# Fourier mixing and a quick-GELU layer on one Trainium2 core: ScalarE's partition moves reissued later, and the first products of a group on one PSUM bank

## The chip, the cores and the metric

The kernel runs on one core of one Trainium2 chip, in one launch. The metric is the device time in microseconds of that core. Before the change three runs took 2061.47, 2064.64 and 2069.29 us; their median is 2064.64 us. The profile shown below is one execution with a span of 2067.7 us.

## The reference

```python
batch, seq, dim = (8, 3008, 256)                     # x, float32
X = np.fft.fft(x, axis=1)
X = np.fft.fft(X, axis=2)
x = X.real.astype(np.float32).reshape(B * S, D)      # 24064 x 256
h = x @ w_in                                         # 256 x 2048
g = h * (1.0 / (1.0 + np.exp(-1.702 * h)))
return (g @ w_out).astype(np.float32)                # 2048 x 256
```

Everything is float32: the real part of a two-dimensional Fourier transform of each of eight samples, and then a layer with one hidden width of 2048 and a sigmoid-weighted activation.

## The kernel before

**What is computed how.** The transform along the sequence (3008 = 47 x 64) is done in two stages by matrix products, with the symmetry of a real input used to halve the work. The transform along the features is folded into the first weight, so that the hidden layer comes out of two products, P with the cosine half of the weight (wcs0) and Q with the sine half (wcs1). Since a row and its mirrored row share P and Q, one pass gives hidden values for both: P + Q forward and P - Q backward. The second layer uses a Winograd form of the 2 x 2 block product: seven products of sums and differences in place of eight. For most of the work two of these seven are split once more in the same way (the "deep" form); the parts of the two are the "small products", which lie in partitions 0 to 63 for the one and 64 to 127 for the other.

**Steps, groups and slots.** The work is a list of 384 steps: 8 samples, 3 blocks each, 2 halves of a block, and 8 steps (NP) in each half, each of which covers 256 of the 2048 hidden columns. The 8 steps of one half accumulate into the same PSUM banks and make a *group*; there are 48 groups. The loop at L906 walks over slots t. In slot t the hidden layer of step t is made, and the second-layer products of step t - 3 (LAG = 3) are issued. So a new group's products begin in the slots with t mod 8 = 3. Below, "slot 3" means a slot with t mod 8 = 3, and so on; slot 3 is the *boundary slot*. The first group (t below 8) is plain, groups 2 to 47 are deep, and the last group is not deep.

**What a slot holds, in the order in which it is issued.** There is no scheduler: each engine's queue has the instructions in the order in which this loop writes them.

- TensorE (all its products but the small ones are issued by the helper at L478): `second(t)` adds Q onto P in the step's bank (8 passes; a float32 product takes two passes, and each is cut into two column halves); `product(t - 3, 0)`, the first two of the five full-size products; `begin(t + 1)`, the next step's P; `product(t - 3, 1)`, the other three; then the small products at L623 (16 passes in even slots, 12 in odd ones).
- ScalarE: `middle(t + 2)`, two scalings (L542); `forward(t)`, the activation of P + Q (L555), which waits for `second(t)`; `activate_back(t - 1)`, the activation of the mirrored half (L562).
- VectorE: `backward(t)` (L503), which makes P - Q; `doubled(t + 1)` (L548), which reads P of the next step and writes 2P plus a row term into SBUF; `second(t + 1)` on TensorE may not add Q before it has done so; then the sums s2 and s4 (L577, L578) and those of the small products (L595).
- GpSimd: the sums s1 and s3 (L574, L575), and in the first third of a sample the folding of the next sample's input (`fold1`, L201 to L206).

`backward(t)` waits for `forward(t)`: both write the same tile h, and both read the same PSUM bank.

**How a group ends.** Five full-size products go to three banks: pot[0] holds (0,0) and (0,1), pot[1] holds (1,0) and (1,1), pot[2] holds (2,0). In the pair, the first number is the bank and the second its half. The small products lie in pot[3] and pot[4].

- `combine(t)`, at the end of slot 2, where the group's last products were issued: ScalarE copies c1 out of pot[0] (L697); four VectorE additions (L703) follow, u2 (reads pot[0]), u3 (reads pot[1]), c (reads pot[1]) and one that reads pot[2].
- `combine_small(t)`, one slot later, at the end of slot 3: ScalarE copies the sum e out of pot[4] (L721); four VectorE additions (L727) combine the small products into the tile held[3]; three ScalarE copies (L728 to L730) exchange a quarter in partitions 0 to 63 with one in partitions 64 to 127.
- `combine_last(t, 0)`, at the end of slot 4: VectorE adds held[3] to the rest (L739), transposes a half (L677) and stores it; `combine_last(t, 1)`, at the end of slot 5, does the other half.

The three banks of the full-size products have no double: the next group's first products in slot 3 go to the banks that `combine` reads. The order of the five products of a step is written out by hand:

```python
plan = [(0, 0, wo[:, p, 0, :], h[:, 0, 0, :n]), (1, 0, wt[:, p, 2, :], s[:, 2, :n]),
        (0, 1, wt[:, p, 1, :], s[:, 1, :n]), (1, 1, wt[:, p, 0, :], s[:, 0, :n]),
        (2, 0, wo[:, p, 3, :], s[:, 3, :n])]
todo = plan[:2] if part == 0 else plan[2:]
```

In some slots more is issued at the end: the next block's second transform stage (L332, with VectorE transposes L338) in slot 0 of every other group, and the next sample's first stage (`mix1`, L230, with two ScalarE copies out of PSUM, L233). In the samples 1 to 6 (counted from 0) `mix1` falls into slots 2 and 6 of the second and third group of the sample. One of its two banks is that of the step just finished, so that it is also the bank of `begin` in the next slot.

Of the kernel before, what the change touches and what calls it, by code (L numbers as in the profile page):

```python
# [43 lines left out]
LAG = 3  # L44
# [67 lines left out]
def kernel(ctx: ExitStack, tc, x, w_in, w_out, tab1, tab2, out):  # L112
    nc = tc.nc
# [29 lines left out]
    wo, wt = wot[:, 0], wot[:, 1]  # L143
# [318 lines left out]
    NP = NF // 2  # L462
    steps = [(b, blk, hh, p) for b in range(B) for blk in range(NBLK) for hh in range(2) for p in range(NP)]
    vb, ht, st, rt, xb, gt, pot = {}, {}, {}, {}, {}, {}, {}
    held = []
    last = len(steps) - NP

    def width(t):

        return 226 if steps[t][1:3] == (0, 1) else 256  # L470
# [52 lines left out]
    def begin(t):  # L523

        n = width(t)
        x = xb[t] = bank("x", f"b{t % 2}")
        for i in range(2):
            halves(x[:, i * 256:i * 256 + n], *operands(t, 0, i), start=(i == 0), stop=False)
# [35 lines left out]
    def sums(t, eng):  # L564

        if not NP <= t < len(steps):
            return
        h, n = ht[t], width(t)
        a11, a12, a21, a22 = h[:, 0, 0, :n], h[:, 0, 1, :n], h[:, 1, 0, :n], h[:, 1, 1, :n]
        if eng is nc.gpsimd:  # L570
            st[t] = held[2] if t % 4 == 3 else sp.tile([128, 4, 256], F32, tag="s", bufs=3, name="s")
        s1, s2, s3, s4 = (st[t][:, q, :n] for q in range(4))
        if eng is nc.gpsimd:
            eng.tensor_tensor(s1, a21, a22, op=ALU.add)  # L574
            eng.tensor_tensor(s3, a11, a21, op=ALU.subtract)  # L575
        else:
            eng.tensor_tensor(s2, s1, a11, op=ALU.subtract)  # L577
            eng.tensor_tensor(s4, a12, s2, op=ALU.subtract)  # L578

    def deep(t):  # L580

        return NP <= t < last
# [16 lines left out]
    def sub(k):  # L599
        q, at = SUBS[k]  # L600
        return pot[q][:, at * 128:(at + 1) * 128]
# [36 lines left out]
    def product(t, part):  # L638

        p, n = steps[t][3], width(t)  # L640
        if part == 0 and p == 0:
            for q in range(2 if t < NP else 3):
                pot[q] = bank(f"po{q}", f"o{q}")
            if t >= NP and not deep(t):
                pot[5] = bank("po5", "b2" if deep(t - 1) else "o3")
        h = ht[t]
        if t < NP:

            plan = [(half, dh, wo[:, p, 2 * f + dh, :], h[:, half, f, :n])
                    for half in range(2) for dh in range(2) for f in range(2)]  # L650
        else:
            s = st[t]
            plan = [(0, 0, wo[:, p, 0, :], h[:, 0, 0, :n]), (1, 0, wt[:, p, 2, :], s[:, 2, :n]),
                    (0, 1, wt[:, p, 1, :], s[:, 1, :n]), (1, 1, wt[:, p, 0, :], s[:, 0, :n]),
                    (2, 0, wo[:, p, 3, :], s[:, 3, :n])]
            if not deep(t):
                plan += [(2, 1, wo[:, p, 2, :], h[:, 0, 1, :n]), (5, 0, wt[:, p, 3, :], h[:, 1, 1, :n])]
        todo = plan[:2] if part == 0 else plan[2:]

        if t >= len(steps) - 2:  # L660
            if part == 0:
                return
            pot[t] = plan
            if t == len(steps) - 2:
                return
            todo = [it for both in zip(pot.pop(t - 1), pot.pop(t)) for it in both]
        begun = set() if p else pot.setdefault("begun", set())
        for q, i, lhs, rhs in todo:
            halves(pot[q][:, i * 256:i * 256 + n], lhs, rhs, start=(p == 0 and q not in begun), stop=(p == NP - 1))
            begun.add(q)  # L670
        if part and p == 0:
            del pot["begun"]
# [7 lines left out]
    def combine(t):  # L680

        b, blk, hh, p = steps[t]
        if p < NP - 1:
            return
        n = width(t)
        o = op.tile([128, 4, 256], F32, tag="os", name="os")
        if t < NP:
            for half in range(2):
                turned(t, o, half, pot[half][:])
            return  # L690
        c = cv.tile([128, 4, 256], F32, tag="m", bufs=2, name="c")
        if n < 256:
            nc.gpsimd.memset(c[:, :, n:], 0.0)
        m = {k: pot[q][:, 256 * i:256 * i + n] for k, q, i in ((6, 0, 1), (7, 1, 0), (5, 1, 1), (3, 2, 0))}
        u = op.tile([128, 3, 256], F32, tag="u", bufs=1, name="u")
        c1, u2, u3 = (u[:, q, :n] for q in range(3))
        nc.scalar.copy(c1, pot[0][:, 0:n])  # L697
        m5 = free(pot[1][:], 256, [0, 2], [1, n])
        plan = [(u2, c1, m[6], ALU.add), (u3, u2, m[7], ALU.add),
                (free(c[:], 256, [512, 2], [1, n]), u[:, 1:3, :n], m5, ALU.add),  # L700
                (c[:, 1, :n], c[:, 1, :n], m[3], ALU.add)]
        for out_, i0, i1, how in plan:
            nc.vector.tensor_tensor(out_, i0, i1, op=how)  # L703
        pot["late"] = o, c, u
        if deep(t):
            return
        for out_, i0, i1, i in ((c[:, 0, :n], c1, pot[2][:, 256:256 + n], 0), (c[:, 2, :n], u3, pot[5][:, 0:n], 1)):
            nc.vector.tensor_tensor(out_, i0, i1, op=ALU.add)
            turned(t, o, i, c[:, 2 * i:])

    def combine_small(t):

        if t < 0 or not deep(t) or steps[t][3] < NP - 1:
            return
        n, w, d = width(t), width(t) // 2, held[3]
        e, saved = d[:, 896:896 + w], d[:, 768:]

        def two_of(ap, at, by):
            return free(ap[:], at, [by, 2], [1, w])

        nc.scalar.copy(e, sub(1)[:, :w])  # L721
        d22 = d[:, 256 + w:256 + 2 * w]
        for out, i0, i1 in ((two_of(d, 0, 512), two_of(d, 896, 0), two_of(pot[3], 0, 128)),
                            (two_of(d, 640, 128), two_of(d, 512, 0), two_of(pot[3], 256, 128)),
                            (two_of(d, 256, w - 256), two_of(d, 640, 128), two_of(pot[4], 0, 128)),
                            (d22, d[:, 768:768 + w], sub(5)[:, :w])):
            nc.vector.tensor_tensor(out, i0, i1, op=ALU.add)  # L727
        nc.scalar.copy(saved[64:128, :n], d[0:64, 256:256 + n])  # L728
        nc.scalar.copy(d[0:64, 256:256 + n], d[64:128, 0:n])  # L729
        nc.scalar.copy(d[64:128, 0:n], saved[64:128, :n])  # L730
# [175 lines left out]
    for t in range(n + LAG):  # L906
        if t < NP:
            hidden(t)
            if t == 0:
                low_up(in2)  # L910
                nyquist(0, 0)
                low_down(in2)
            if t in rows_at:
                first_row(rows_at[t])
            if t >= LAG:
                for part in range(2):
                    product(t - LAG, part)
            if t in early:
                fold_w(early[t])
            if t:  # L920
                activate(t - 1)
            rows(t)
            if t == NP - 1:
                for ahead in range(2):
                    middle(NP + ahead)
                begin(NP)
        else:
            if t < n:
                if t + 2 < n:
                    middle(t + 2)  # L930
                second(t)
            product(t - LAG, 0)
            if t + 1 < n:
                begin(t + 1)
            product(t - LAG, 1)
            small_products(t - LAG, (1, 2, 4, 7))
            small_products(t - LAG - 1, (5, 6, 3))
            if t == NP:
                activate(t - 1)
            if t < n:  # L940
                forward(t)
            if NP < t <= n:
                activate_back(t - 1)
                sums(t - 1, nc.gpsimd)
            if t < n:
                backward(t)
        if NP <= t + 1 < n:
            doubled(t + 1)
        if t >= NP:
            sums(t - 2, nc.vector)  # L950
            deeper(t - 2, 0)
            deeper(t - 3, 1)
        if t >= LAG:
            combine(t - LAG)
            combine_small(t - LAG - 1)
            combine_last(t - LAG - 2, 0)
            combine_last(t - LAG - 3, 1)
        if t == NP:
            held += [hp.tile(shape, F32, tag="h", name="held") for shape in
                     ([128, 2, 4, 2, 64], [128, 2, 4, 2, 64], [128, 4, 256], [128, 1024])]  # L960
        if t >= NP:
            spare[:] = ["b2", f"b{t % 2}"]
        for fn, args in extra.get(t, ()):
            fn(*args)
# [28 lines left out]
```

## Time and profile before

| engine | busy us | share of the span |
|---|---|---|
| TensorE matmuls (PE) | 1928.9 | 93% |
| TensorE weight loads (PEld) | 1399.4 | 68% |
| VectorE (DVE) | 1548.5 | 75% |
| ScalarE (ACT) | 875.3 | 42% |
| GpSimd (POOL) | 796.1 | 38% |

The span is 2067.7 us, with 51061 instructions; the mean granted TensorE clock is 0.986 of full speed. The DMA engines are lightly used (51 GB/s on average). The busy time of PE is modelled from pipelined matmuls, so that a span in which PE never waits shows as fully busy; the missing 7% are the time in which it stood.

The chain of work that ended last is followed back from the last instruction, at each step to what released it. By engine it consists of PE 70%, DVE 17%, ACT 7% and a small rest. Where it leaves PE, PE stood and another engine's work set the time.

### The profile page before, as it was taken

What the parts mean: (1) busy time and instruction counts of PE and PEld (TensorE: products, weight loads), DVE (VectorE), ACT (ScalarE), POOL (GpSimd) and SP (SyncE); (2) the same over time, 40 slices, a digit from 0 to 9 for tenths busy, and PEclk for the clock granted to TensorE, in tenths of its full rate; (3) what the DMA queues carried; (4) which work ended last, traced back from release to release, by engine and by line L of the source; (5) the groups of instructions that cost most, each with busy time, mean ns of one, the idle gap of its engine ahead of it and who ended that gap; (6) DMA issues with size and microseconds to landing.
All of it is one profiled execution on the core that took longest, in us unless ns stands there. A gap on an engine that the chain in (4) does not pass through costs nothing.

```text
span 2067.7 us, 51061 instructions
## 1 busy us (share of the span) xinstructions
PE 1928.9 (93%) x21392; PEld 1399.4 (68%) x21392; DVE 1548.5 (75%) x3011; ACT 875.3 (42%) x1868; POOL 796.1 (38%) x1073
## 2 busy tenths in 40 slices
PE   8989999989998999999999999999999999999998
PEld 5666677667676676666666666666666666677665
DVE  7667778777788777787778777788777877777775
ACT  6533434444444444444444344434444444444442
POOL 4474224532245322452225522255222642322232
PEclk9999999999999999999999999999999999999999
DMA  8623151236220352204513054031631222202201
GB/s 284 130 45 43 51 81 14 44 46 112 17 35 23 53 106 17 47 16 75 81 15 52 16 100 54 12 57 39 95 31 22 17 44 44 26 13 17 20 18 22
DMA packets 145399, 104.93 MB, mean 51 GB/s; under 512 B 104914, under 2 KB 127986, under 8 KB 143984
## 3 DMA queue, kind: packets, MB, share of 16 engines
q1 hardware_dynamic: 143952, 101.14, 29.3%
q8 instruction: 168, 2.75, 0.6%
q10 hardware_dynamic: 1216, 0.52, 0.1%
q14 instruction: 63, 0.52, 0.1%
HBM read 58.38 MB, written 48.01 MB: 51 GB/s over the span
## 4 chain that ended last, share of the span: by engine, by line
PE 70%; DVE 17%; ACT 7%; issue 2%; DMA 1%; POOL 1%; SPq 1%; DVEq 0%; ACTq 0%; POOLq 0%
PE po L478 31%; PE x L478 26%; PE po L623 10%; DVE r L595 3%; DVE held L727 3%; DVE g L548 3%; ACT g L542 2%; DVE h L503 2%; ACT h L555 1%; DVE c L703 1%; PE ps L230 1%; PE ps L332 1%; DVE s L577 1%; DVE u L703 1%; ACT held L729 1%
## 5 line engine op out<-in xcount | busy, mean ns | idle before, releaser
L478 PE MATMUL x<-pq,wcs 128*64 128x256 f32 (+1 forms) x6016 | 789.1, 382 | 84.5 <-DVE g L548 82.3
L478 PE MATMUL po<-s,wo 128*64 128x256 f32 (+1 forms) x4512 | 586.5, 379 | 27.8 <-DVE c L703 25.3
L478 PEld LDWEIGHTS x<-pq,wcs 128*64 128x64 f32 x6016 | 433.6, 139 | 260.5 <-DVE g L548 94.5
L555 ACT ACTIVATE h<-x 128x512 f32<-128x512 f32 (+1 forms) x376 | 220.2, 586 | 749.9 <-PE x L478 729.8
L574 POOL TENSOR_TENSOR s<-h 128x256 f32<-128x256 f32 (+1 forms) x282 | 204.9, 727 | 792.9 <-issue 460.8
L503 DVE TENSOR_TENSOR h<-g,x 128x512 f32<-128x512 f32 (+2 forms) x440 | 254.5, 590 | 330.2 <-ACT h L555 329.5
L478 PEld LDWEIGHTS po<-s,wo 128*64 128x64 f32 x4512 | 344.0, 139 | 178.9 <-issue 40.9
L542 ACT ACTIVATE g<-nb,af 128x256 f32<-128x256 f32 (+1 forms) x752 | 335.1, 495 | 1.4 <-DVE h L512 0.8
L548 DVE SCALAR_TENSOR_TENSOR g<-x,g 128x512 f32<-128x512 f32 (+1 forms) x376 | 254.4, 677 | 95.0 <-PE x L478 94.7
L478 PE MATMUL po<-h,wo 128*64 128x256 f32 (+1 forms) x1824 | 267.6, 382 | 2.5 <-DVE u L703 2.2
L562 ACT ACTIVATE h<-h 128x512 f32<-128x512 f32 (+1 forms) x376 | 230.9, 614 | 0.2 <-DVE h L503 0.2
L574 POOL TENSOR_TENSOR held<-h 128x256 f32<-128x256 f32 (+1 forms) x94 | 69.9, 744 | 404.1 <-ACT h L562 319.3
L575 POOL TENSOR_TENSOR s<-h 128x256 f32<-128x256 f32 (+1 forms) x282 | 206.6, 733 | 0.0
L595 DVE TENSOR_TENSOR r<-h 128x256 f32<-128x256 f32 (+1 forms) x368 | 195.8, 573 | 0.0
L478 PE MATMUL po<-held,wo 128*64 128x256 f32 (+1 forms) x1504 | 193.0, 375 | 0.0
L623 PE MATMUL po<-r,held 128*64 128x128 f32 (+1 forms) x2208 | 184.4, 270 | 0.0
L478 PEld LDWEIGHTS po<-h,wo 128*64 128x64 f32 x1824 | 134.5, 138 | 71.7 <-DVE u L703 17.8
L577 DVE TENSOR_TENSOR s<-s,h 128x256 f32<-128x256 f32 (+1 forms) x282 | 168.8, 598 | 3.1 <-POOL s L574 3.1
L623 PEld LDWEIGHTS po<-r,held 128*64 128x64 f32 x2208 | 143.4, 137 | 22.0
L578 DVE TENSOR_TENSOR s<-h,s 128x256 f32<-128x256 f32 (+1 forms) x282 | 147.8, 524 | 9.7
L478 PEld LDWEIGHTS po<-held,wo 128*64 128x64 f32 x1504 | 110.8, 137 | 49.0
L623 PE MATMUL po<-h,wo 128*64 128x128 f32 (+1 forms) x1472 | 112.1, 271 | 2.5 <-DVE held L727 2.2
(106 smaller groups left out, 1700.8 us busy)
## 6 DMA issues: line engine op xcount, KB each, us to landing
out_dram<-os SPq DMA_DIRECT2D x284, 64.0 KB
Td<-xt SPq DMA_DIRECT2D x14, 768.0 KB
t<-Td SPq DMA_DIRECT2D x7, 1536.0 KB
xt<-in_x_dram SPq DMA_DIRECT2D x14, 512.0 KB
xt<-Xr SPq DMA_DIRECT2D x14, 512.0 KB
nb<-pq SPq DMA_DIRECT2D x23, 256.0 KB
out_dram<-os SPq DMA_DIRECT2D x96, 56.0 KB
Xr<-in_x_dram SPq DMA_DIRECT2D x7, 752.0 KB
```

What stands on the lines that cost most here:

```text
L478: nc.tensor.matmul(out[c0:c0 + 64], lhsT=lhs[:, c0:c0 + 64], rhs=rhs, skip_group_check=True, **how)
L503: nc.vector.tensor_tensor(free(h[:], 512 + at + m - 1, [256, 2], [RUN, blocks], [-1, m]), *ins, op=op)
L542: nc.scalar.activation(g[:, i * 256:i * 256 + n], nbt[b, blk][:, hh * 256:hh * 256 + n], ACTF.Copy, scale=af2[:, f:f + 1])
L548: nc.vector.scalar_tensor_tensor(g, two(xb[t][:], n), 2.0, g, op0=ALU.mult, op1=ALU.add)
L555: nc.scalar.activation(two(h[:], n), two(xb[t][:], n), ACTF.Gelu_apprx_sigmoid)
L562: nc.scalar.activation(g, g, ACTF.Gelu_apprx_sigmoid)
L574: eng.tensor_tensor(s1, a21, a22, op=ALU.add)
L575: eng.tensor_tensor(s3, a11, a21, op=ALU.subtract)
L577: eng.tensor_tensor(s2, s1, a11, op=ALU.subtract)
L578: eng.tensor_tensor(s4, a12, s2, op=ALU.subtract)
L595: nc.vector.tensor_tensor(out, i0, i1, op=how)
L623: nc.tensor.matmul(sub(k)[64 * side:64 * side + 64, :w], lhsT=lhs, rhs=rhs, start=(p == 0 and k in (1, 2)), stop=(p == NP - 2), skip_group ...
```

## The change

Three edits. First, in `combine_small` the copy of e moves forward: it is now issued in `combine`, one slot earlier, behind the copy of c1. Second, the three exchanging copies get a function of their own, `swap`, which is called one slot later than before, behind that slot's `forward` and `activate_back`, and ahead of `backward`. Third, the five products of a step are reordered so that the first two both go to pot[0], and in a boundary slot `begin(t + 1)` is issued ahead of `product(t - 3, 0)`. The first two edits are for ScalarE: its queue should not stand at the copies while activations wait behind them. The third is for TensorE: it should not stand at pot[1] while VectorE still reads it. No instruction is added or removed, and every engine has the same instructions as before, in another order on TensorE and ScalarE; the order on VectorE, GpSimd and SyncE does not change.

```diff
-            plan = [(0, 0, wo[:, p, 0, :], h[:, 0, 0, :n]), (1, 0, wt[:, p, 2, :], s[:, 2, :n]),
-                    (0, 1, wt[:, p, 1, :], s[:, 1, :n]), (1, 1, wt[:, p, 0, :], s[:, 0, :n]),
+            plan = [(0, 0, wo[:, p, 0, :], h[:, 0, 0, :n]), (0, 1, wt[:, p, 1, :], s[:, 1, :n]),
+                    (1, 0, wt[:, p, 2, :], s[:, 2, :n]), (1, 1, wt[:, p, 0, :], s[:, 0, :n]),
                     (2, 0, wo[:, p, 3, :], s[:, 3, :n])]
...
         if deep(t):
+            nc.scalar.copy(held[3][:, 896:896 + n // 2], sub(1)[:, :n // 2])
             return
...
-        nc.scalar.copy(e, sub(1)[:, :w])
         d22 = d[:, 256 + w:256 + 2 * w]
...
             nc.vector.tensor_tensor(out, i0, i1, op=ALU.add)
+
+    def swap(t):
+
+        if t < 0 or not deep(t) or steps[t][3] < NP - 1:
+            return
+        n, d = width(t), held[3]
+        saved = d[:, 768:]
         nc.scalar.copy(saved[64:128, :n], d[0:64, 256:256 + n])
         nc.scalar.copy(d[0:64, 256:256 + n], d[64:128, 0:n])
         nc.scalar.copy(d[64:128, 0:n], saved[64:128, :n])
...
-            product(t - LAG, 0)
-            if t + 1 < n:
-                begin(t + 1)
+            heads = [(product, t - LAG, 0)] + [(begin, t + 1)] * (t + 1 < n)
+            for fn, *args in heads[::-1] if t >= NP + LAG and (t - LAG) % NP == 0 else heads:
+                fn(*args)
             product(t - LAG, 1)
...
                 activate_back(t - 1)
                 sums(t - 1, nc.gpsimd)
+            swap(t - LAG - 2)
             if t < n:
                 backward(t)
```

More of the change, by code (lines that the diff above doesn't have):

```diff
@@ L714, in combine_small @@
             return
-        n, w, d = width(t), width(t) // 2, held[3]
-        e, saved = d[:, 896:896 + w], d[:, 768:]
+        w, d = width(t) // 2, held[3]
         def two_of(ap, at, by):
             return free(ap[:], at, [by, 2], [1, w])
-        nc.scalar.copy(e, sub(1)[:, :w])
         d22 = d[:, 256 + w:256 + 2 * w]
```

## The prediction

> **What bounds the kernel now.** I read the page first. PE is busy 93% of the span and heads the chain of work with 70%, so the question is where the other 30% of the chain lie. The list of waits gives the times in which PE stood, and for whom:
>
> ```profile
> ACT held L728 <- DVE held L727: 101.6, 46, 4.1
> ...
> PE x L478 <- DVE g L548: 82.3, 52, 3.0
> ...
> PE po L478 <- DVE c L703: 25.3, 40, 0.7
> ```
>
> Columns: total us, times, longest us. PE stood 107.6 us in two places, about once in each of the 46 ends of a deep group (46 is the count of L728). Then the chain of waits, in order of time, over one such end:
>
> ```profile
> 1037.70 0.43 DVE u L703
> ...
> 1038.15 0.70 DVE c L703
> ...
> 1038.99 0.65 PE po L478 x4
> ...
> 1042.49 0.28 ACT held L721
> ...
> 1044.47 0.41 ACT held L728
> ...
> 1045.76 0.91 ACT g L542 x2
> 1046.66 0.49 ACT h L555
> ...
> 1047.18 0.69 DVE h L503
> 1047.87 0.61 DVE g L548
> ```
>
> Columns: start us, us, what. Twice the chain leaves PE. *Stall A*, in boundary slot 3: product (1,0) waits until c has been read out of pot[1]. *Stall B*, in slot 4: ScalarE stands at the exchanging copies (L728 waits for L727); behind them in its queue are `middle` and `forward`; VectorE waits for `forward`, and PE for VectorE's `doubled`. Last, windows cut at the starts of slots 3 and 4, in an ordinary group and in one with `mix1` (its slots 4 and 5):
>
> ```profile
> 1036.60:1042.25 5.65, 4.95 (x52) 3.41 (x50) 4.76 (x11) 1.12 (x2) 1.41 (x2) 1.00 0.38 16
> 1042.25:1048.52 6.27, 4.96 (x56) 3.94 (x52) 3.25 (x9) 4.18 (x10) 0.72 (x2) 1.00 0.02 4
> ...
> 914.33:922.29 7.96, 4.96 (x58) 3.83 (x53) 5.10 (x10) 4.09 (x10) 3.78 (x5) 0.95 0.00 0
> 922.29:929.81 7.52, 7.52 (x48) 4.53 (x50) 5.74 (x11) 1.91 (x4) 5.01 (x7) 0.60 0.15 32
> ```
>
> Columns: length, then busy us of PE, PEld, DVE, ACT, POOL, then clock, DMA share, GB/s. An undisturbed odd slot is 0.86 + 0.86 + 0.86 + 1.29 + 0.67 = 4.54 us by the chain's own pieces; the even slot 2 before this boundary took 4.76. So A costs 5.65 - 4.54 = 1.11 us and B 6.27 - 4.76 = 1.51 us, restart of the pipeline included. In the mix group B is longer, and after a 3.00 us stop the clock is down to 0.60 in slot 5.
>
> **What the Trainium skill says.** "PSUM — Partial Sum Buffer", section "PSUM bank collisions raise a hardware error", wants PSUM guarded by bank and quadrant, not by address: this is why (1,0) waits for c, and why giving the first two products to pot[0] alone moves the wait from c to u2. The trace agrees: (0,0) started at 1037.65, when u2 was made, and (1,0) 1.34 us later. The same page, "Engine vs sequencer instructions", calls the queues of ScalarE and VectorE strictly first in, first out; stall B is that. "TensorE: Matmul & The Clock Gate", section "What's actually happening", has the clock at half after an idle window of some 3.4 us; the trace shows 0.60 after a stop of 3.00 us and 1.00 after the 1.31 us of the ordinary B. "SBUF — State Buffer", section "Who interferes with whom", says that a VectorE operation with two SBUF inputs contends with GpSimd's reads; here L595 takes 494 ns for 256 columns on average but 948 ns for 226, whose groups coincide with GpSimd's folding.
>
> **The change part by part**, in times after the start of slot 3 (1036.60 in the ordinary case). No instruction is added, so no work is priced, only waits and margins.
>
> *Products on one bank, behind P (stall A).* PE: `second` to 0.86, `begin` to 1.72, (0,0) and (0,1) to 2.58, then (1,0). VectorE works without a break from 1034.65 on, so its times stand: u2 at 1.05, c at 2.25, the reader of pot[2] at 2.76, where PE arrives at 3.44. All three are in time, the tightest by 0.33 us. Product (0,1) now needs s2 in every slot, 1.29 us after `second` begins (0.43 more in slot 3, and 0.86 for P); s2 is VectorE's next operation after the `doubled` that releases `second`, and takes 0.4 to 0.8, 1.1 at worst. So no new wait: A's 1.11 us go. `begin` in front needs the bank of step t - 1, which VectorE left 2 us earlier; behind it wait only the products.
>
> *Copy of e one slot earlier.* It waits for the small products of slot 2 and so ends at about 0.3; behind it ScalarE has `middle` (0.91), so `forward` starts at 1.25 in place of 1.08. VectorE is in `combine` until 2.76, which hides it. In return L727 loses the copy's 0.28 us ahead of it.
>
> *The exchange one slot later (stall B).* VectorE: `backward` from 2.76 to 3.4, `doubled` to 4.05 (PE's next `second` is due at 4.54), sums to 4.9, L595 to 5.6, L727 (1.60 for four) to 7.2. ScalarE in slot 4: `forward` from 5.5 to 6.1, `activate_back` to 6.7, then it waits for L727 and copies from 7.2 to 8.5. VectorE: `backward` (0.69) and `doubled` (0.61) from 7.2 to 8.5; PE wants that at 4.54 + 4.76 = 9.30. Margin 0.8 us, B's 1.51 go. The small products of slot 4, which overwrite what L727 reads, come at 8.4: margin 1.2. The added wait, L739 on the exchange, has `backward` and `doubled` of slot 5 behind it on VectorE, and PE behind these; VectorE gets there after its sums at 10.5, 2 us after the copies' end, so it costs nothing.
>
> *Ordinary boundaries:* 46 less 12 with `mix1` = 34, times 2.62 = 89 us. Check: 34 x (0.68 + 1.31) us of standing = 68, which leaves 40 of the 107.6, or 3.3 each, for the other 12; the long B of the window says the same.
>
> *The 12 mix boundaries.* Here `mix1`'s copies (L233) keep `forward` of slot 3 until 911.8, and GpSimd's folding stretches two L595 to 2.36. From `backward` at 911.82 VectorE has 0.69 + 0.6 + 0.82 + 0.35 + 2.36 + 1.48 (L727) + 0.69 + 0.61 = 7.6 us, so `doubled` ends at 919.4 in place of 922.25. PE is there at about 918.8: `begin`, now in front, must wait some 0.4 us (and a 0.2 restart) for the L233 copy that holds its bank until 910.50. So 0.6 us of stop remain, and the saving is 2.9; in the other of the two kinds the same sum gives 2.6. I take 2.7: 12 x 2.7 = 32 us. The stop is too short for the clock to fall. The clock's loss is (1 - 0.986) x 2068 = 29 us, of which start and end have about 5; of the other 24 I count 15, since VectorE would have bound some of the slow slots anyway.
>
> *Sum:* 89 + 32 + 15 = 136 us. I take 4 off for small new waits (0.1 in each boundary): 2064.6 - 132 = 1932 us.
>
> **The rivals.** *VectorE becomes the bound.* It is busy 4.76 + 3.25 + 4.49 = 12.5 us in slots 3 to 5, against 13.89 for PE undisturbed. GpSimd's two additions of a slot can double an operation with two SBUF inputs (0.41 to 0.8); in a new phase three more of them would use up 1.2 us against margins of 0.33 and 0.8. For: the margins are small. Against: in the windows shown these operations are already hit once a slot, and after slot 5 VectorE catches up. It would leave about 1 us at each of 46 boundaries: 1932 + 46 = 1978.
>
> *Only A goes.* If `swap` held ScalarE as long as before, or L739 took over the wait, B would stay. Then 34 x 1.1 and some of the mix groups: 2064.6 - 45 = 2020. For: the copies still wait for L727 in ScalarE's queue. Against: `forward` and `activate_back` are now in front, and only the next `middle` is behind, due 2 us later.
>
> *Slower.* `begin` in front waits for L233 or a backlog on VectorE in every boundary, and L739 holds VectorE for the whole exchange in slot 4, with `doubled` behind it; if both cost 1.5 us where A and B cost 2.6 and the freed stalls came back one slot later, the kernel would end at 2064.6 + 46 x 0.4 = 2083. The margins above speak against it.
>
> **How the numbers follow.** Both stalls gone 0.70, VectorE bound 0.17, only A 0.09, slower 0.04. The time is that of the likeliest, 1932. The lowest that the trace allows is 2064.6 less 112 us of standing (both waits, with 4.4 on u and L727), some 20 of restarts (92 x 0.2) and 24 of clock: 1909. The low end is 1911, and the upper end 1985, to take in VectorE as the bound; the other two cases, 0.13, stay outside with a little of the first. Faster by over 0.5%: 0.95; the same 0.02; slower 0.03.
>
> **What would show it.** In the profile after, "PE po <- DVE c" and L728's wait ahead of `forward` should be gone, "PE x <- DVE g" should fall from 82 to 20 us or less, PE should rise to 97 or 98%, and ordinary slots 3 and 4 should take 4.5 and 4.8 us. Slot 3 at 4.9 or more would say that (1,0) or `begin` waits; slot 5 longer than 4.7, that L739 does. A clock that still falls in the mix groups would leave 15 us. The prediction is wrong if VectorE's busy time grows by more than a few per cent through contention with GpSimd.

## The result and the profile after

The changed kernel takes 1927.78 us (median of four runs, 1925.14 to 1927.89) against 2066.86 us before (median of four: the three runs named at the start and one of 2069.08): a ratio of 0.9327, with a 95% interval of 0.9305 to 0.9350. The forecast was 1932 us.

In the list of waits of the changed kernel (total us, times, longest us), the two lines that were stall A and stall B read as follows. L734 and L726 are the L728 and L727 of before, and the line "PE po <- DVE c" is gone from the list.

```profile
ACT held L734 <- DVE held L726: 17.0, 22, 1.3
...
PE x L478 <- DVE g L548: 4.6, 7, 0.8
```

PE stood 107.6 us for VectorE in these two places; 4.6 are left. The exchange still waits for L726, now and then, but with nothing behind it that is due. The chain of waits over the same stretch of an ordinary group (start us, us, what), from the `second` of slot 3 to the end of slot 4, no longer leaves PE:

```profile
1007.49 1.73 PE x L478 x16
1009.22 2.16 PE po L478 x20
1011.38 0.66 PE po L623 x12
...
1015.92 0.87 PE po L623 x16
```

The first line is `second` and the `begin` drawn in front of the products, 16 passes in one piece; the second is all five products; the pieces left out are PE's as well. Then the windows (length, busy us of PE, PEld, DVE, ACT, POOL, then clock, DMA share, GB/s): slots 3 and 4 of this ordinary group, and slots 4 and 5 of a mix group of the same kind as the one shown of before.

```profile
1007.32:1011.86 4.54, 4.54 (x52) 3.25 (x50) 4.23 (x10) 2.98 (x7) 1.43 (x2) 1.00 0.00 2
1011.86:1016.62 4.76, 4.76 (x56) 3.46 (x54) 4.59 (x12) 3.23 (x7) 1.43 (x2) 1.00 0.02 3
```

```profile
858.97:863.73 4.76, 4.76 (x57) 3.46 (x55) 4.62 (x10) 2.44 (x6) 4.35 (x6) 1.00 0.00 0
863.73:868.27 4.54, 4.54 (x53) 3.24 (x51) 4.40 (x10) 2.64 (x6) 2.19 (x4) 1.00 0.12 27
```

Both boundary slots are down to an undisturbed slot: 5.65 and 6.27 us became 4.54 and 4.76. In the mix group 7.96 and 7.52 became 4.76 and 4.54, and the clock stays at 1.00 where it was 0.60. The page's first part says the same for the whole span; the chain is 83% PE in place of 70%.

```profile
PE 1892.3 (98%) x21392; PEld 1376.7 (71%) x21392; DVE 1549.2 (80%) x3011; ACT 875.6 (45%) x1868; POOL 786.5 (41%) x1073
```

VectorE's busy time did not grow (1548.5 before, 1549.2 after). PE's fell by 36.6 us, though it has the same 21392 passes: fewer of them ran at the low clock (mean granted clock 0.986 before, 0.996 after), and fewer began again after a stop (the four passes behind stall A took 0.65 us; four in the run of 20 above take 0.43).

If the span is cut at the first pass of each `second`, the 141.6 us by which the profiled span fell (2067.7 to 1926.1) divide into 90.5 us in the 34 groups with an ordinary boundary, 50.4 us in the 12 mix groups (those whose boundary has a `mix1`) and 0.8 us elsewhere, each rounded.

### The profile page after: what moved, and what is told of

Read it like the earlier page. It is cut to its first block, busy times and chain, and to the rows that moved or that the text cites. A ratio compares the mean times of both kernels' runs of the same rounds, so it can differ in the third digit from the quotient of the medians.

```text
span 1926.1 us, 51018 instructions
## 1 busy us (share of the span) xinstructions
PE 1892.3 (98%) x21392; PEld 1376.7 (71%) x21392; DVE 1549.2 (80%) x3011; ACT 875.6 (45%) x1868; POOL 786.5 (41%) x1073
## 4 chain that ended last, share of the span: by engine, by line
PE 83%; DVE 11%; ACT 3%; POOL 1%; issue 1%; DMA 0%; SPq 0%; DVEq 0%; ACTq 0%; POOLq 0%
PE po L478 37%; PE x L478 29%; PE po L623 12%; DVE r L595 4%; DVE h L503 2%; DVE g L548 1%; PE ps L332 1%; PE ps L230 1%; DVE s L577 1%; DVE s L578 1%; ACT xt L233 1%; DVE held L577 1%; PE ps L283 1%; ACT g L542 1%; DVE os L677 1%
## 5 line engine op out<-in xcount | busy, mean ns | idle before, releaser
L478 PE MATMUL x<-pq,wcs 128*64 128x256 f32 (+1 forms) x6016 | 771.5, 377 | 9.0 <-DVE g L548 4.6
L555 ACT ACTIVATE h<-x 128x512 f32<-128x512 f32 (+1 forms) x376 | 221.5, 589 | 793.1 <-PE x L478 697.3
L478 PE MATMUL po<-s,wo 128*64 128x256 f32 (+1 forms) x4512 | 571.6, 375 | 3.0 <-DVE s L577 1.9
L478 PEld LDWEIGHTS x<-pq,wcs 128*64 128x64 f32 x6016 | 426.7, 137 | 180.8 <-issue 12.3
L478 PEld LDWEIGHTS po<-s,wo 128*64 128x64 f32 x4512 | 334.0, 137 | 150.6 <-DVE s L577 2.3
L595 DVE TENSOR_TENSOR r<-h 128x256 f32<-128x256 f32 (+1 forms) x368 | 205.1, 598 | 0.0
L578 DVE TENSOR_TENSOR s<-h,s 128x256 f32<-128x256 f32 (+1 forms) x282 | 133.3, 473 | 9.7
```

The source lines that it names most:

```text
L478: nc.tensor.matmul(out[c0:c0 + 64], lhsT=lhs[:, c0:c0 + 64], rhs=rhs, skip_group_check=True, **how)
L555: nc.scalar.activation(two(h[:], n), two(xb[t][:], n), ACTF.Gelu_apprx_sigmoid)
L595: nc.vector.tensor_tensor(out, i0, i1, op=how)
```

## The experiments

All are the changed kernel with one thing put back, moved or multiplied, unless the text says otherwise. "After" in what follows is the changed kernel, which took 1928.24 us when it was run once more beside the first two kernels of the last part, on the mix groups (ratio 0.9347, 0.9333 to 0.9361). Each ratio is to runs of the kernel before made beside it (medians from 2063.62 to 2067.09 us), so kernels that were not run side by side are best compared by their ratios.

### Each half of the change alone

Products and P in the new order, ScalarE's copies where they were:

```diff
         if deep(t):
-            nc.scalar.copy(held[3][:, 896:896 + n // 2], sub(1)[:, :n // 2])
             return
...
+        nc.scalar.copy(d[:, 896:896 + w], sub(1)[:, :w])
         d22 = d[:, 256 + w:256 + 2 * w]
...
-            swap(t - LAG - 2)
...
             combine_small(t - LAG - 1)
+            swap(t - LAG - 1)
```

> The third edit alone (products reordered, P ahead in the boundary slot); the copy of e and the exchange stay where they were before. My theory: the two stalls lie one behind the other, so this edit alone is worth less than stall A's 1.11 us. PE leaves slot 3 after 4.54 us, but VectorE still ends L727 7.2 us after the slot's start (its own work, not the copy of e, sets this), the exchange ends at 8.5, the scalings at 9.4, the activation at 10.0, P - Q at 10.6 and `doubled` at 11.2: slot 4 grows from 6.27 to about 6.7, and an ordinary boundary gains 0.67, not 1.11 us. 34 x 0.67 = 23 us and nothing in the mix groups, whose clock still falls: 2067 - 23 = 2044 us. Rival, each edit takes its own stall: slot 4 stays at 6.27 and the time is 2067 - 34 x 1.11 = 2029 us.

Measured: 2024.76 us, ratio 0.9819 (0.9791 to 0.9846). The time alone would speak for the rival's 2029, but the windows of an ordinary group do not: slot 3 lost its stall and slot 4 grew.

```profile
1051.05:1055.59 4.54, 4.54 (x52) 3.25 (x50) 4.23 (x10) 1.11 (x2) 1.42 (x2) 1.00 0.01 2
1055.59:1062.12 6.53, 4.93 (x56) 3.39 (x52) 3.60 (x10) 4.18 (x10) 0.72 (x2) 1.00 0.01 3
```

And the chain over another ordinary boundary of this kernel shows why: VectorE comes to L726 straight from its own sums, and no copy of e and no PE stands ahead of it.

```profile
1016.79 0.67 DVE r L595 x2
1017.46 0.34 DVE held L726
...
1018.35 0.63 DVE held L726 x2
...
1019.06 0.41 ACT held L734
...
1022.45 0.61 DVE g L548
```

So an ordinary boundary gained 1.11 us in slot 3 and gave back 0.26 in slot 4, 0.85 in all: between my 0.67 and the rival's 1.11. L726 ended sooner than I had put it (at 1018.98, when slot 3 had begun at 1012.05: after 6.9 us, not 7.2). Over all 34 of these groups the profiled run gained 29 us. Its span is another 19 us shorter, of which 17.5 are in the mix groups, mostly from a clock that fell less often there (0.994 in the profiled run; over the four, 0.994 and 0.995 in the two runs of 2021 and 2023 us, 0.990 and 0.989 in those of 2027 and 2031). Neither theory had foreseen that.

The moves on ScalarE alone, products and P in the old order:

```diff
-            plan = [(0, 0, wo[:, p, 0, :], h[:, 0, 0, :n]), (0, 1, wt[:, p, 1, :], s[:, 1, :n]),
-                    (1, 0, wt[:, p, 2, :], s[:, 2, :n]), (1, 1, wt[:, p, 0, :], s[:, 0, :n]),
+            plan = [(0, 0, wo[:, p, 0, :], h[:, 0, 0, :n]), (1, 0, wt[:, p, 2, :], s[:, 2, :n]),
+                    (0, 1, wt[:, p, 1, :], s[:, 1, :n]), (1, 1, wt[:, p, 0, :], s[:, 0, :n]),
...
-            heads = [(product, t - LAG, 0)] + [(begin, t + 1)] * (t + 1 < n)
-            for fn, *args in heads[::-1] if t >= NP + LAG and (t - LAG) % NP == 0 else heads:
-                fn(*args)
+            product(t - LAG, 0)
+            if t + 1 < n:
+                begin(t + 1)
```

> The first two edits alone (e early, exchange one slot later), with the products and P in the old order. My theory: stall B goes wholly, since slot 3 stays at 5.65 us and VectorE then has even more time: slot 4 4.76, slot 5 4.54. 34 x 1.51 = 51 us from ordinary boundaries, and nearly all of the mix groups' gain (about 50 us, the clock no longer falls): about 1967 us. PE waits for `c` about 25 us, as before. Rival, stall B returns in part as a wait of L745 for the exchange or of slot 5: slot 4 or slot 5 over 5 us and a time over 1990.

Measured: 1977.7 us, ratio 0.9580 (0.9562 to 0.9599). The windows of slots 3 and 4 of an ordinary group, and the line of waits for stall A:

```profile
1033.36:1039.03 5.67, 4.98 (x53) 3.50 (x50) 4.78 (x11) 2.98 (x7) 1.42 (x2) 1.00 0.00 1
1039.03:1043.79 4.76, 4.76 (x57) 3.99 (x55) 4.31 (x11) 3.23 (x7) 1.43 (x2) 1.00 0.01 3
```

```profile
PE po L478 <- DVE c L703: 25.3, 40, 0.7
```

Stall A is there as before, to the tenth of a microsecond, and stall B is gone. The time is 11 us over my 1967, which had the mix groups gain some 50 us; they gained 40 (slot 4 takes 5.74 us there in the one kind, against 4.49 after). The two halves bring 39.8 and 86.9 us by their medians, 126.7 together; the change brings 139 (135 in the later comparison). Part of the difference is what the first half gives back as long as the second is missing: 34 x 0.26 = 9 us.

### Which part of the new order counts

The new order of products without P ahead:

```diff
-            heads = [(product, t - LAG, 0)] + [(begin, t + 1)] * (t + 1 < n)
-            for fn, *args in heads[::-1] if t >= NP + LAG and (t - LAG) % NP == 0 else heads:
-                fn(*args)
+            product(t - LAG, 0)
+            if t + 1 < n:
+                begin(t + 1)
```

> After, but P of the next step stays behind the first two products in the boundary slot. Theory: (0,0) comes at 0.86 us, u2 is made at 1.05: a wait of 0.2 and a restart of 0.2 at each ordinary boundary; (1,0) then comes after P at about 2.9, behind `c` at 2.25. 34 x 0.4 = +14 us, less 12 x 0.4 in the mix groups, where P no longer waits for the copy out of its bank: 1928 + 9 = 1937 us, ordinary slot 3 at 4.9 us. Rival, the new order alone is enough: within 4 us of 1928.

And P ahead without the new order of products (only the `plan` lines of the diff above put back):

> After, but the products in their old order, (0,0), (1,0), (0,1), (1,1), (2,0), with P ahead of them in the boundary slot. Theory: (0,0) comes at 1.72 us, (1,0) at 2.15, `c` ends at 2.25: a wait of 0.1 and a restart of up to 0.2 at each ordinary boundary, 34 x 0.25 = +8: 1936 us, ordinary slot 3 at 4.8 us. Rival, P ahead alone is enough: within 4 us of 1928, slot 3 at 4.6 or less.

Measured: 1942.19 us (ratio 0.9408, 0.9391 to 0.9425) and 1938.33 us (0.9389, 0.9373 to 0.9406). Slot 3 of an ordinary group, first of the one, then of the other:

```profile
1014.11:1018.88 4.77, 4.76 (x52) 3.15 (x50) 4.46 (x11) 2.98 (x7) 1.43 (x2) 1.00 0.00 2
```

```profile
1011.78:1016.59 4.81, 4.76 (x53) 3.65 (x51) 4.50 (x11) 2.98 (x7) 1.42 (x2) 1.00 0.00 2
```

Each alone leaves 0.23 to 0.27 us of the 1.11, so each takes about four fifths of stall A, and only both take it wholly. In the first, (0,0) comes 0.2 us before u2; in the second (1,0) comes 0.1 us before `c`. What I had expected the first to win back in the mix groups, because P no longer waits for L233 there, did not come. Their slot 3 fell to 4.14 and 4.52 us, but slot 4 of the one kind grew from 4.49 to 5.73 us, where PE now waits for VectorE (0.79 us for L726, 0.34 for `doubled`), and slot 6 of the other from 5.88 to 6.50, for a reason that stays open. In all, the mix groups lost 4.5 us.

### Which of ScalarE's moves counts

The exchange one slot later, the copy of e left in `combine_small` (the first two hunks of the first diff above):

> After, but the copy of e stays in `combine_small`, at the end of slot 3, ahead of L726. Theory: the copy waits for PE's end of slot 3 (4.55 us after its start) and ends at 4.83, but VectorE gets to L726 only at about 5.4, from its own sums; on ScalarE the next activation is 0.25 us later than in after, and P - Q waits for L726 anyway. So moving e is worth nothing once the exchange is behind the activations: within 5 us of 1928, ordinary slot 4 at 4.76. Rival, L726 is held by e: 46 x 0.28 = +13, 1941 us.

Measured: 1930.45 us (ratio 0.9348, 0.9323 to 0.9373), and in the profile slots 3 and 4 of 4.54 and 4.76 us, as after. The reverse, e early and the exchange at the end of slot 3 (the last two hunks of that diff):

> After, but the exchange stays at the end of slot 3 (e is early, products and P in the new order). Theory: all of stall B comes from the place of the exchange: as with the products alone, slot 4 at 6.5 us and about 2025 us. Rival, the early copy of e takes part of stall B: slot 4 at 6.2 or less, 2015 us or less.

Measured: 2025.98 us (ratio 0.9807, 0.9783 to 0.9832), the time of the products alone. Its slot 4:

```profile
1058.01:1064.53 6.52, 4.93 (x57) 3.39 (x53) 3.59 (x10) 3.91 (x9) 0.73 (x2) 1.00 0.01 3
```

So the early copy of e is worth nothing that can be measured, with the exchange moved or without; VectorE's own sums set the start of L726. Next, whether the place in the slot matters: the exchange in slot 4, but ahead of `forward`.

```diff
                 activate(t - 1)
+            swap(t - LAG - 2)
             if t < n:
                 forward(t)
             if NP < t <= n:
                 activate_back(t - 1)
                 sums(t - 1, nc.gpsimd)
-            swap(t - LAG - 2)
```

> After, but the exchange is issued one place earlier: in slot 4 ahead of `forward`, not behind `activate_back`. `middle` is still in front of it. Theory: what counts is whether `forward` is queued behind the exchange. It then starts at about 8.35 us after slot 3's start (L726 ends at 7.0, three copies), P - Q ends at 9.6, `doubled` at 10.2, PE wants it at 9.3: slot 4 at 5.9 us. 34 x 1.1 = 37 us, in the mix groups some 1.7 each, 20 us: about 1986 us. Rival, one slot later is enough, whatever the place in it: 1928 us.

Measured: 1990.43 us (ratio 0.9639, 0.9610 to 0.9668). The chain over an ordinary boundary:

```profile
1005.30 0.41 ACT held L734
...
1006.60 0.60 ACT h L555
...
1007.92 0.61 DVE g L548
...
1008.57 1.08 PE x L478 x8
```

The exchange is followed by `forward` (L555) with no scalings between, and about two thirds of stall B are back: slot 4 takes 5.74 us, 0.98 of the 1.51 more than after. So it is not the slot but what is queued behind the exchange. Last, its slack: each copy three times.

```diff
-        nc.scalar.copy(saved[64:128, :n], d[0:64, 256:256 + n])
-        nc.scalar.copy(d[0:64, 256:256 + n], d[64:128, 0:n])
-        nc.scalar.copy(d[64:128, 0:n], saved[64:128, :n])
+        for _ in range(3):
+            nc.scalar.copy(saved[64:128, :n], d[0:64, 256:256 + n])
+            nc.scalar.copy(d[0:64, 256:256 + n], d[64:128, 0:n])
+            nc.scalar.copy(d[64:128, 0:n], saved[64:128, :n])
```

> After, with the exchange done three times over (9 copies in place of 3; the same data in the end). Theory: behind the activations the exchange has slack. Nine copies take about 3.9 us and end at 10.9; VectorE gets to L745 at 10.4, the next `forward` comes at 11.8 in place of 10.3, `doubled` ends at 13.7 and PE wants it at 13.84: hidden in ordinary groups, up to 0.5 us in some of the others: 1928 to 1936 us. Rival, the exchange is still on the chain that sets the end: 46 x 2.6 = +120, 2048 us.

Measured: 1933.62 us (ratio 0.9362, 0.9338 to 0.9387). In the list of waits (L746 is L745 of after, L737 the last copy):

```profile
DVE c L746 <- ACT held L737: 47.7, 45, 1.6
...
PE x L478 <- DVE g L548: 14.7, 20, 1.2
```

VectorE now waits a microsecond at each end of a group, but PE hardly does; ordinary groups are unchanged and the 12 mix groups lost about 0.6 us each. Six more copies of 0.4 us, 46 times, are 110 us of ScalarE's work that cost about 5.

### What is left: the mix groups

Two of the mix groups' slots are long in after: slot 3, where P in front waits for a copy of `mix1`, and slot 6 of the sample's second group. In the first kernel ScalarE empties the bank that P needs first, by turning `for r in range(2)` around L233 into `for r in (1, 0)`.

> After, with the two ScalarE copies (L233) of every `mix1` in turned order, so that the bank that P of the next step needs is emptied first. Theory: in after, P in front waits in the 12 mix boundaries until the second copy ends (0.2 to 0.3 us of standing and a restart; slot 3 takes 4.94 and 4.65 us there in place of about 4.54 and 4.15). With the turned order P comes after the first copy, which ends about when `second` does: 12 x 0.45 = 5 us less, 1922 to 1924 us. Rival, the wait moves into slot 4 because VectorE binds there: no change.

Measured: 1923.28 us, ratio to before 0.9323 (0.9308 to 0.9337), beside 1928.24 us and 0.9347 (0.9333 to 0.9361) of after itself. The medians are 5 us apart, as expected, though the intervals overlap a little. Slot 3 fell from 4.65 and 4.94 to 4.14 and 4.52 us; slot 4 gave back 0.1 to 0.2. That the sum is what I had expected is partly luck: in the sample's third groups slot 6 grew from 5.88 to 6.50 us and slot 0 fell from 5.21 to 4.41. I had foreseen neither, and the causes stay open.

The second kernel adds a delay of the second `mix1` of a sample by one slot, out of the long slot 6:

```diff
-                    at(t0 + 8 + 2 * c + late, mix1, b + 1, c // 2)
+                    at(t0 + 8 + 2 * c + late + (c == 3 and b > 0), mix1, b + 1, c // 2)
```

> As the kernel with turned copies, and the second of the four `mix1` of a sample (slot 6 of the sample's second group) one slot later. Theory: in after this slot takes 6.71 us and not 5.33, since the second bank of `mix1` waits for P - Q, with VectorE behind on its sums, which GpSimd's folding stretches. One slot later VectorE has caught up: 6 x 1.3 = 8 us less, about 1915 us. Rival, VectorE is behind in the next slot as well: 1922 us or more.

Measured: 1928.19 us (ratio 0.9345, 0.9331 to 0.9359): not faster but 5 us slower than without this move. My reading was wrong. Slot 6 after the move:

```profile
827.00:833.15 6.15, 4.53 (x57) 3.23 (x53) 6.12 (x9) 1.81 (x4) 3.73 (x5) 1.00 0.19 40
```

Slot 6 has no `mix1` now and is still 6.15 us long, with VectorE busy for 6.12 of them: VectorE is the bound there, and `mix1` had only stood in the gap. Slot 7, which has `mix1` now, grew from 4.17 to 5.29 us. The timeline of VectorE in after shows what holds it (start us, us). These operations were issued in slot 5, but nearly all of them run in slot 6, which PE began at 828.15:

```profile
827.88 1.40 DVE L577 TENSOR_TENSOR held<-held,h 128x226 f32<-128x226 f32 x1
...
830.04 2.47 DVE L595 TENSOR_TENSOR r<-h 128x226 f32<-128x226 f32 x2
```

During the first 2.8 of these 4.6 us GpSimd folds the next sample's input (L201 to L206, 827.47 to 830.71), and then it makes its own two sums, until 831.96. So the third kernel, which keeps the turned copies, leaves `mix1` out of slots 6 and 7 and moves that folding:

```diff
-                at(t0 + 7 + 2 * c + late, fold1, b + 1, c, nc.gpsimd)
+                at(t0 + 7 + 2 * c + late + (c == 3 and b > 0), fold1, b + 1, c, nc.gpsimd)
...
-                    at(t0 + 8 + 2 * c + late, mix1, b + 1, c // 2)
+                    at(t0 + 8 + 2 * c + late + 2 * (c == 3 and b > 0), mix1, b + 1, c // 2)
```

> As the kernel with turned copies, with the fourth `fold1` of a sample (GpSimd, slot 5 of the sample's second group) one slot later, and the second `mix1`, which needs it, two slots later (slot 0 of the next group). My theory after the kernel with a later `mix1`: it is not `mix1` that makes slot 6 long in these groups but VectorE, whose L577, L578 and L595 in slot 5 are stretched from 1.6 to 4.7 us by GpSimd's folding, on top of L745 and the two transposes. Away from slot 5 the folding meets a VectorE that is ahead: slot 6 then takes about 4.3 us, and slot 0 behind it 5.5 with the products of `mix1`; 6 x 1.35 = 8 us less, about 1915 us. Rival, the folding stretches as much wherever it stands, and VectorE falls behind one slot later: 1923 us or more, with slot 7 or 0 longer by what slot 6 loses.

Measured: 1917.4 us, ratio to before 0.9280 (0.9265 to 0.9296), the fastest of all the kernels here, and clear of the 0.9308 to 0.9337 of the turned copies alone. The same operations in its timeline, and its slot 6:

```profile
823.51 0.37 DVE L577 TENSOR_TENSOR held<-held,h 128x226 f32<-128x226 f32 x1
...
824.23 0.69 DVE L595 TENSOR_TENSOR r<-h 128x226 f32<-128x226 f32 x2
```

```profile
823.79:828.00 4.21, 4.21 (x57) 3.38 (x55) 3.97 (x11) 1.81 (x4) 2.01 (x4) 1.00 0.39 84
```

4.6 us became 1.4, and slot 6 4.21. The folding now stretches the operations that are issued in slot 6 (an L595 took 1.46 us), but there VectorE has time in hand.

## Why the prediction was right

**The path.** Both stalls were what the chain of waits said. Each vanishes with its own half of the change and stays without it.

**Stall A.** Predicted 1.11 us for each ordinary boundary; measured 1.11 in most, 1.14 on average. That u2 and `c` keep their times, since VectorE works without a break, held; the margin of 0.33 us for (1,0) was real, for P ahead alone (0.43 less) misses it by 0.1. That the wait is for the bank can be seen in the kernel: `c` reads only the other half of pot[1], (1,1), and yet (1,0) waited for it. Product (0,1), which now needs s2 earlier, waited for it once in the whole run (1.9 us).

**Stall B.** Predicted 1.51 us; measured 1.51 in most and 1.45 on average, and 0.05 more in slot 5. In six of the 34 slot 4 still takes 5.18 us: those are the slots in which `rotate`, one small product for the next sample, is issued. The step "the exchange one slot later" carried all of the gain. The step that gave the copy of e 0.28 us was without effect, as its own working implied: L726 starts at VectorE's time, not at e's. The margin that I gave as 2 us for L739 (L745 of after) was smaller: from the end of the last copy to the start of L745 there were 1.6 us in the median ordinary group and 1.2 to 1.4 in the mix groups. The threefold exchange, 2.6 us longer, used it up and made L745 wait by about 1 us, and only the 12 mix groups felt it.

**Ordinary boundaries.** 34 x 2.62 = 89 us predicted, 90.5 measured.

**Mix boundaries and the clock.** 32 + 15 = 47 us predicted, 50.4 measured. The trace of before separates the two terms, for behind three of its twelve stops of 3 us the clock did not fall: in the third group of samples 1 and 5 and in the second group of sample 6, counted from 0. Here is one of each kind over its eight slots, and below them the same two groups in after (columns as in the windows above):

```profile
393.18:436.11 42.93, 39.11 (x437) 28.17 (x434) 36.68 (x61) 18.90 (x41) 25.28 (x34) 1.00 0.13 26
1604.62:1648.09 43.47, 39.62 (x506) 29.82 (x504) 36.44 (x71) 18.06 (x41) 25.71 (x36) 1.00 0.25 20
```

```profile
374.60:414.33 39.73, 38.90 (x437) 27.39 (x434) 35.56 (x61) 18.92 (x41) 24.37 (x33) 1.00 0.14 28
1494.29:1534.90 40.61, 39.54 (x506) 29.69 (x504) 36.22 (x71) 18.06 (x41) 25.37 (x36) 1.00 0.27 21
```

With the clock at 1.00 throughout, a third group gained 3.2 us and a second group 2.9. Taken over six of each (in after all third groups last 39.7 us, and the second ones 40.6 to 40.8) that is 36 us, against the 32 that I had put. The other 14 us go to the clock, against 15. So the total was not met by two errors that cancel.

In the first term, the 0.6 us of stop that I left in slot 4 did not come (4.76 us in the window): the two L595 took 1.82 us in place of the 2.36 that I had copied from before, and operations of VectorE overlap by some hundredths each, so that 7.6 us of work were 6.84. The slot-3 wait of P for L233 was there, as predicted (12 times, 3.0 us, and the restarts).

In the second term, I had counted 15 of 24 us because VectorE would have bound some of the slow slots anyway, and it did so in a slot that I had not looked at. Slot 6 of the sample's second group took 5.33 us in five of the six groups of before, but 6.57 already in the one whose clock had not fallen, and 6.71 in most of after, 7.0 us more in all. That was the rival "VectorE becomes the bound", with GpSimd's folding in the place of its two additions: I had let VectorE catch up after slot 5.

**The clock.** The mean granted clock rose from 0.986 to 0.996, which is 29 us of loss against 8; in the mix groups of after it did not fall once.

**The sum.** The parts came to 136 us. The 4 us that I took off for small new waits were not needed, and the time ended 4 us below the forecast.

**The rivals.** "Only A" came to 2025 us when tried, near its 2020, but not by its sum: the ordinary groups gained 29 us and not 37, and the mix groups 17.5. "Slower" had the wait of L739 as its ground, and that wait had more than 1 us to spare in nearly every group.

## What to carry to other kernels

In a strict queue, what counts is less what an operation costs than what stands behind it while it waits: 2.6 us of extra copies behind the activations cost nearly nothing, while the same three copies one place ahead of an activation cost 1 us at each boundary. Where two stalls lie one behind the other, removing the first alone gives part of its time back in the second, so read which engine would be late next before adding up. And once the main engine no longer stands, look for slots in which a helper's work (here GpSimd's folding) meets the longest stretch of the second-busiest engine, and move it to a slot where that engine waits anyway.

## What the hardware did that was not expected

A stop shorter than 3 us can bring the TensorE clock down, and where it lies decides. In every trace here, all falls of the clock lie a whole number of steps of 3.413 us apart, and a low stretch inside the span lasts one or two such steps. In before, for example, low stretches begin at 375.30, 627.89 and 672.26 us, 74 steps and 13 steps from one to the next. In the kernel with the exchange ahead of `forward`, PE stops for 2.15 us in the second group of each of six samples. In three of them the whole stop falls into one step, and the next step runs at half the clock; in the other three it is divided between two steps, and the clock stays at 1.00. One of each kind, cut at the steps (clock is the third number from the end, PE's busy time the second of the line):

```profile
845.04:848.45 3.41, 1.26 (x16) 0.82 (x14) 2.24 (x6) 2.38 (x6) 1.44 (x2) 1.00 0.02 5
848.45:851.86 3.41, 3.41 (x20) 2.19 (x18) 3.15 (x8) 1.81 (x4) 2.20 (x4) 0.50 0.07 16
```

```profile
1083.97:1087.39 3.42, 2.42 (x34) 1.82 (x30) 1.32 (x5) 1.89 (x5) 1.09 (x2) 1.00 0.02 7
1087.39:1090.80 3.41, 2.25 (x24) 1.74 (x26) 3.34 (x8) 2.42 (x6) 1.58 (x3) 1.00 0.03 5
```

The 3 us stops of before follow the same rule: behind nine of the twelve the clock fell, and in the three others no step held more than 1.94 us of the stop. Cut in this way, the traces of this case have 25 falls between the first 140 us and the end of the last product. In the step ahead of each, PE was idle for 1.98 us or more of the 3.41; no step at the full clock with 1.97 or less was followed by one. PE's ends are modelled, so the border is only known as about 2 us. "TensorE: Matmul & The Clock Gate", section "What's actually happening", speaks of an idle window of about 3.4 us that does not start with the kernel but runs freely. The fixed steps agree with that, but the window need not be idle throughout. The stop of 1.3 us in the ordinary groups of before never brought the clock down.

VectorE's operations with two SBUF inputs lost more beside GpSimd than the factor of two that I had put for its two additions: the pair of L595 over 226 columns took 2.47 us beside the end of the folding and these additions, and 0.69 us when the folding was moved, a factor of 3.6. The prediction had 2.36 us for such a pair from the trace of before, but not what it takes undisturbed. Nor are all L595 of these groups stretched: the 948 ns of the prediction are the mean of one of three forms, and the other two over 226 columns took 446 and 442 ns in before. The page "SBUF — State Buffer", section "Who interferes with whom", names the contention; these runs give its size for this pair.
